# Attention on one core: the order of a round's instructions, and eight sets of split heads

## The chip, the cores and the metric

One NeuronCore of a Trainium2 chip. The metric is the device time of one execution in microseconds (us). Five engines work beside each other, each in the order of its own instruction stream: TensorE (PE, with its weight loads shown as PEld), VectorE (DVE), ScalarE (ACT), GpSimd (POOL) and SyncE (SP, which only issues DMAs here). Semaphores tie them together where one reads what another writes.

## The reference

Attention with 4 batches, 8 heads, 576 positions, 64 dimensions a head; then a mixture of eight experts with the two best per token, then a dense layer pair with a leaky activation.

```python
scores = scale * np.matmul(q, k.transpose(0, 1, 3, 2))
thresh = np.max(scores, axis=-1, keepdims=True) - tau
scores = np.where(scores >= thresh, scores, -1000000000.0)
attn = np.exp(scores - max); attn = attn / (sum + 1e-09)
x = np.matmul(attn, v)                          # 2304 tokens x 512
x = sum over the two best experts of weight * (relu(x @ w1[e]) @ w2[e])
h = x @ w_in
out = (max(h, 0) + alpha * min(h, 0)) @ w_out
```

## The kernel before, in words

Heads go in pairs: the two heads of a pair fill the 128 partitions, 64 each. Attention is cut into 80 units of (batch b, row block c, head pair hp). A full unit is 128 query rows of two heads, so it has two score matrices of 128 x 576; a "t" unit is the last or first 64 rows of both heads put in one 128-row matrix. Units 0 to 15 are batch 0 by head pair, then by block; after them a tile of 128 tokens takes four consecutive units, one for each head pair. Units 16 to 23 and 56 to 63 are the "t" units.

Scores are computed from q and k split into a high and a low part (fp32r), three products each (`s_mm`, L333 to L347). The split parts of one head pair are a *set*; `split_hi` (L285, ScalarE copy), `split_lo` (L293, GpSimd subtraction in two halves, and for q the four small copies of `tail_tile`, L277) fill it. Six sets lie in six buffers; the list `sched` (L639 to L648) says at which round each part is split, and after each split the next raw part is loaded by a DMA on SP (`next_load`).

A unit goes through these steps:

- scores on TensorE into the PSUM ring `s` (two buffers, one for each head);
- `d1` (L358) on VectorE: scale, write to SBUF, row minimum of the negated scores;
- `a1` (L369) on ScalarE: the exponential; `thresh` (L363): the threshold;
- `d2` (L382) on VectorE: the mask times the exponential, with its row sum;
- `t_mm` (L399 to L403) on TensorE: transposes of 4, 4 and 1 blocks into the PSUM ring `t` (three buffers); `a2` (L411 to L415) on ScalarE: copies of them to SBUF;
- `pv` on TensorE into the single PSUM buffer `v`: 16 products on half the array's columns (L434) and one on the whole array for the last 64 positions (L436); for "t" units L429 and L430.

The order is written out by hand in one loop (L714 to L757). Round i issues the scores, `d1`, `a1` and `thresh` of unit i, `d2` of unit i-1, transposes and copies of unit i-2 and `pv` of unit i-3. When the fourth head pair of a tile is done, its result is copied out (`group_evac`, L460), and in the following rounds come the tile's stages: rows (four transposes L475, then on VectorE an addition, a reciprocal and the scaling L471 to L477, and a DMA), logits (L485 and the copy L488), flip (one transpose L492), and the sum of the logits (L496 and L499 on VectorE). All but the sum stand at the end of a round (phase 1); the sum stands at phase 0. They use the ring `t` too. Later rounds hold the gating of two or three tiles at a time (L520 to L576), and the sends of tokens by GpSimd's DMAs (L594).

From round 66 on the first expert's weights are split in the same loop (L170, L173). After the last unit, pieces of the first expert block (`do_fill`) fill the drain. The expert layers that follow are TensorE products in three terms (L197, L215).

Of the kernel before, what the change touches and what calls it, by code (L numbers as in the profile page):

```python
# [4 lines left out]
FT = mybir.dt.float32  # L5
FR = mybir.dt.float32r
# [8 lines left out]
HP = H // 2  # L15
# [8 lines left out]
NSET = 6  # L24
DT = 2
# [7 lines left out]
def emit(tc, qt, kt, v, tau, wg, wn, noise, w1, w2, w_in, w_out, alpha, out):  # L33
# [8 lines left out]
    with (  # L42
# [47 lines left out]
        m_pair = [mem.tile([128, 4096], FR, name=f"m_pair{i}") for i in range(NSET)]  # L90
# [58 lines left out]
        for p, k in ((4, 3), (5, 5), (2, 7), (3, 9), (0, 11), (1, 13)):  # L149
            slots(m_pair[p], k, k + 1)  # L150
# [6 lines left out]
        X0 = (cut(m_pair[0], 0, [HP, 256], FR), cut(m_pair[0], 1024, [HP, 256], FR))  # L157
        H0 = (cut(m_pair[0], 2048, [8 * 256], FR), cut(m_pair[1], 0, [8 * 256], FR))
# [108 lines left out]
        def pair(n):  # L267

            c = Cuts(m_pair[n % NSET])
            return [c([S], FR), c([S], FR), c([KW], FR), c([KW], FR), c([128], FR), c([128], FR)]  # L270
# [148 lines left out]
        def pv(i):  # L419
            b, c, hp = units[i]  # L420
            u = st[i]
            P = u["P"]
            if hp == 0 or i < SOLO:
                vps["v"] = psum_v()
            o = vps["v"][:, hp * 128:hp * 128 + 128]
            V, BD = vt[b % 2], vbd[b % 2]
            if c == "t":
                for j in range(4):
                    pe.matmul(o, V[:, j, hp * 128:hp * 128 + 128], P[:, j], start=(j == 0), stop=False)  # L429
                pe.matmul(o, V[:64, 4, hp * 128:hp * 128 + 128], P[:64, 8], start=False, stop=True)  # L430
            else:
                for j in range(4):
                    for h in range(2):
                        pe.matmul(o[h * 64:h * 64 + 64], V[:, j, hp * 128 + h * 64:hp * 128 + h * 64 + 64],  # L434
                                  P[:, 4 * h + j], start=(j == 0), stop=False, skip_group_check=True)
                pe.matmul(o, BD[:, hp], P[:, 8], start=False, stop=True, skip_group_check=True)  # L436
            st[i].clear()
# [203 lines left out]
        for b in range(1, B):  # L641
            o = 20 * b
            for j, (dt, part) in enumerate(((-12, "q"), (-10, "k"))):
                sched.append((o + dt, 4 * b, part, pool))
            for j, (dt, part) in enumerate(((-8, "q"), (-6, "k"))):
                sched.append((o + dt, 4 * b + 1, part, pool))
            sched += [(o - 4, 4 * b + 2, "q", pool), (o - 3, 4 * b + 2, "k", pool),
                      (o - 1, 4 * b + 3, "q", pool), (o, 4 * b + 3, "k", pool)]  # L648
            put(o - 9, load_v, b)
# [63 lines left out]
        END = NU + DT + 1  # L713
        for i in range(END):  # L714
            it = i - DT
            tiles = 0 <= it < NU
            if i < NU:
                s_mm(i)
                for h in range(nh(i)):
                    d1(i, h)  # L720
                for h in range(nh(i)):
                    a1(i, h)
                thresh(i)
            else:
                do_fill()
# [3 lines left out]
            if tiles:  # L729
                t_mm(it, 0)  # L730
                a2(it, 0)
            for f, a in at.pop((i, 0), []):
                f(*a)
# [3 lines left out]
            iv = it - 1  # L737
            if 0 <= iv < NU:
# [12 lines left out]
            if tiles:  # L751
                t_mm(it, 2)
                a2(it, 2)
# [212 lines left out]
        ca, cb, cc = [Cuts(mem.tile([128, 4096], FT, name=f"m_pair{i}")) for i in range(3)]  # L966
# [104 lines left out]
```

## Time and profile before

| what | value |
|---|---|
| median of 3 runs (lowest to highest) | 1247.83 us (1243.76 to 1247.86) |
| profiled execution, its own time | 1247.19 us |
| span of the profile | 1245.1 us |
| TensorE busy | 1189.1 us, 96% of the span |
| VectorE, ScalarE, GpSimd busy | 610.9, 545.3, 510.7 us |
| mean granted TensorE clock | 0.993 |
| a raw k part's load (320 KB), issue to landing | 4.6 us |

How to read it: busy shares are means over stages with different limits, so the rows below are taken by stretch. "Idle before, releaser" is how long an engine stood before an instruction, and what ended it; "issue" means that nothing in the profile did. Matmuls overlap one another, so the start of weight loads (PEld) is the better clock for TensorE's order.

### The profile page before, as it was taken

What the parts mean: (1) busy time and instruction counts of PE and PEld (TensorE: products, weight loads), DVE (VectorE), ACT (ScalarE), POOL (GpSimd) and SP (SyncE); (2) the same over time, 40 slices, a digit from 0 to 9 for tenths busy, and PEclk for the clock granted to TensorE, in tenths of its full rate; (3) what the DMA queues carried; (4) which work ended last, traced back from release to release, by engine and by line L of the source; (5) the groups of instructions that cost most, each with busy time, mean ns of one, the idle gap of its engine ahead of it and who ended that gap; (6) DMA issues with size and microseconds to landing.
All of it is one profiled execution on the core that took longest, in us unless ns stands there. A gap on an engine that the chain in (4) does not pass through costs nothing.

```text
span 1245.1 us, 21730 instructions
## 1 busy us (share of the span) xinstructions
PE 1189.1 (96%) x8422; PEld 1047.5 (84%) x8422; DVE 610.9 (49%) x1413; ACT 545.3 (44%) x1109; POOL 510.7 (41%) x609
## 2 busy tenths in 40 slices
PE   7998888988889999999999999999999999999996
PEld 6887666777678899999999898998998998998995
DVE  7967787778844333333535342352442442442340
ACT  7967667766724444344444354442221221221220
POOL 6542542562333445443544444544431441441330
PEclk9999999999999999999999999999999999999998
DMA  6332222123143655554645455541111110110100
GB/s 206 99 101 91 99 89 72 69 76 121 50 166 132 209 176 182 177 181 175 220 169 201 163 178 170 193 146 51 35 35 34 42 39 23 43 43 18 43 10 19
DMA packets 60603, 135.27 MB, mean 109 GB/s; under 512 B 9680, under 2 KB 10320, under 8 KB 60496
## 3 DMA queue, kind: packets, MB, share of 16 engines
q1 hardware_dynamic: 54448, 114.61, 27.3%
q0 software_dynamic: 5760, 18.88, 4.5%
q8 instruction: 68, 1.11, 0.4%
q14 instruction: 39, 0.32, 0.1%
q10 hardware_dynamic: 288, 0.34, 0.1%
HBM read 93.96 MB, written 39.85 MB: 107 GB/s over the span
## 4 chain that ended last, share of the span: by engine, by line
PE 83%; ACT 5%; DVE 5%; issue 4%; POOL 1%; DMA 1%; SPq 0%; ACTq 0%; DVEq 0%; POOLq 0%
PE ps_t L197 33%; PE ps_s L215 33%; PE ps_s L347 6%; PE ps_t L399 2%; ACT m_hh L369 2%; DVE m_tmp L358 2%; PE ps_v L434 2%; DVE m_hh L382 1%; PE ps_t L186 1%; ACT sm L363 1%; ACT m_tmp L411 1%; PE ps_v L436 1%; PE ps_v L186 1%; ACT m_last L411 1%; PE ps_t L475 1%
## 5 line engine op out<-in xcount | busy, mean ns | idle before, releaser
L215 PE MATMUL ps_s<-m_pair,m_hh 128*128 128x512 f32 x1032 | 338.4, 395 | 0.0
L197 PE MATMUL ps_t<-m_v,m_pair 128*128 128x256 f32 (+1 forms) x2016 | 290.6, 295 | 2.5 <-DVE m_gate L208 2.5
L197 PEld LDWEIGHTS ps_t<-m_v,m_pair 128*128 128x128 f32 x2016 | 275.8, 191 | 3.8 <-DVE m_gate L208 2.7
L215 PEld LDWEIGHTS ps_s<-m_pair,m_hh 128*128 128x128 f32 x1032 | 193.9, 188 | 39.9
L942 POOL TENSOR_TENSOR m_gate<-m_tmp,m_hh 128x256 fp32r<-128x256 f32 x144 | 105.0, 741 | 249.1 <-ACT m_hh L941 248.1
L215 PE MATMUL ps_s<-m_pair,m_gate 128*128 128x512 f32 x516 | 201.7, 391 | 0.0
L173 POOL TENSOR_TENSOR m_pair<-m_v,m_pair 128x1024 fp32r<-128x1024 f32 x55 | 135.7, 2469 | 141.8 <-ACT m_pair L170 128.0
L197 PE MATMUL ps_t<-m_v,m_early 128*128 128x256 f32 (+1 forms) x1152 | 174.8, 296 | 1.3 <-ACT m_v L189 0.8
L197 PEld LDWEIGHTS ps_t<-m_v,m_early 128*128 128x128 f32 x1152 | 161.7, 191 | 3.0 <-ACT m_v L189 1.1
L369 ACT ACTIVATE m_hh<-m_tmp,sm 128x576 f32<-128x576 f32 x144 | 105.4, 774 | 89.6 <-DVE m_tmp L358 89.4
L382 DVE SCALAR_TENSOR_TENSOR m_hh<-m_tmp,sm,m_hh 128x576 f32<-128x576 f32 x144 | 133.2, 957 | 0.0
L358 DVE TENSOR_SCALAR_CACHE_REDUCE m_tmp<-ps_s 128x576 f32<-128x576 f32 x144 | 103.9, 754 | 58.8 <-PE ps_s L347 58.3
L208 DVE SCALAR_TENSOR_TENSOR m_gate<-ps_t,m_hh 128x384 fp32r<-128x384 f32 (+1 forms) x120 | 58.3, 493 | 151.3 <-ACT m_hh L207 151.3
L938 DVE TENSOR_SCALAR m_tmp<-ps_t,alpha_t 128x256 f32<-128x256 f32 x144 | 69.7, 484 | 117.1 <-PE ps_t L197 117.0
L941 ACT CAST m_hh<-m_tmp 128x256 fp32r<-128x256 f32 x144 | 58.0, 406 | 144.9 <-DVE m_tmp L939 144.9
L215 PEld LDWEIGHTS ps_s<-m_pair,m_gate 128*128 128x128 f32 x516 | 97.1, 188 | 18.3 <-DVE m_gate L208 0.2
L347 PE MATMUL ps_s<-m_pair 64*128 64x288 f32 (+1 forms) x864 | 90.2, 321 | 7.1 <-ACT m_pair L628 4.4
L207 ACT ACTIVATE m_hh<-ps_t 128x384 fp32r<-128x384 f32 (+1 forms) x120 | 52.2, 440 | 93.9 <-PE ps_t L197 92.8
L347 PEld LDWEIGHTS ps_s<-m_pair 64*128 64x128 f32 (+1 forms) x864 | 70.2, 195 | 19.4 <-issue 5.6
L399 PE MATMUL ps_t<-ident,m_hh 128*128 128x128 f32 x576 | 82.7, 284 | 1.1 <-ACT m_last L411 0.4
L299 POOL TENSOR_TENSOR m_pair<-m_early,m_pair 128x288 fp32r<-128x288 f32 (+1 forms) x60 | 54.5, 929 | 59.1 <-ACT m_pair L289 37.7
L399 PEld LDWEIGHTS ps_t<-ident,m_hh 128*128 128x128 f32 x576 | 64.4, 143 | 12.8 <-issue 7.4
(200 smaller groups left out, 1435.6 us busy)
## 6 DMA issues: line engine op xcount, KB each, us to landing
m_v<-in_w_dram SPq DMA_DIRECT2D x64, 512.0 KB, 3.9
yg<-m_tmp SPq DMA_DIRECT2D x40, 256.0 KB, 2.6
m_tmp<-in_w_in_dram SPq DMA_DIRECT2D x16, 512.0 KB, 4.9
m_tmp<-in_w_out_dram SPq DMA_DIRECT2D x16, 512.0 KB, 4.7
m_v<-xg SPq DMA_DIRECT2D x20, 256.0 KB, 4.5
m_rows<-xg SPq DMA_DIRECT2D x20, 256.0 KB, 4.1
m_early<-in_kt_dram SPq DMA_DIRECT2D x15, 320.0 KB, 4.6
yg<-m_gate SPq DMA_DIRECT2D x18, 256.0 KB, 2.1
```

The lines of the kernel that those rows point to most:

```text
L173: eng.tensor_tensor(WL[n], wraw.pop(n), f32(WH[n]), op=OP.subtract)
L197: pe.matmul(ps[:, :n], w[wc[d]][:, col:col + 128], x[xx][:, d, :n], start=(k == 0), stop=(k == 11))
L208: dve.scalar_tensor_tensor(hs[1][:, f * n:f * n + n], ps, 0.0, f32(h), op0=OP.max, op1=OP.subtract)
L215: pe.matmul(ps, a[:, o:o + 128], ww[w][:, c:c + 512], start=(f == 0 and k == 0), stop=(f == nf - 1 and k == 2))
L347: pe.matmul(u["ps", h][:, x, :288], lhs, kk[r, o:o + 288], start=(k == 0), stop=(k == 2))
L358: dve.tensor_scalar(u["sp"][:, h].rearrange("p (a b) -> p a b", a=2), ps[:, :, :288], -0.125, None, op0=OP.mult, op1=OP.min, accum_out=u[" ...
L369: act.activation(u["em"][:, h], u["sp"][:, h], AF.Exp, bias=u["sm"][:, h:h + 1], scale=-1.0)
L382: dve.scalar_tensor_tensor(u["em"][:, h], u["sp"][:, h], sm[:, 2 + h:3 + h], u["em"][:, h], op0=OP.is_le, op1=OP.mult, accum_out=acc)
L399: pe.transpose(ps[:, j * 128:j * 128 + 128], emf[:, o + j * 128:o + j * 128 + 128], ident)
L938: dve.tensor_scalar(t_, ps, 0.0, alpha_t[:, f:f + 1], op0=OP.min, op1=OP.mult)
L941: act.copy(h, g_)
L942: pool.tensor_tensor(hl[:, f * 256:f * 256 + 256], g_, f32(h), op=OP.subtract)
```

## The change

Each round is written in another order. The scores of unit i+1 are issued in round i, after the transposes of unit i-2; the first scores stand ahead of the loop. The first four transposes and their copy come first in the round, ahead of the minimum and the exponentials; the other two copies come after the exponentials, and the threshold after those. `pv` is cut in two: its whole-array product (`pv_tail`) starts the accumulation between the second and the last transposes, and the 16 half-array products follow after the next scores. Phase 0 moves behind the scores.

The split parts get eight sets, in one buffer, of 2688 words each; the splits of the later batches are put into earlier rounds, one round or two apart. The weight slots and the first expert block's inputs are laid out anew in the same buffer.

```diff
@@ -21,7 +21,8 @@
 CAP = 640
 TAIL = 512
 KW = S + S - TAIL
-NSET = 6
+NSET = 8
+SETW = 2688
 DT = 2
 BLOCK0 = 256
 FIRST = 12
@@ -87,7 +88,7 @@
                 return self.aps[self.i % len(self.aps)]
 
         m_early = mem.tile([128, 6 * 1024], FT, name="m_early")
-        m_pair = [mem.tile([128, 4096], FR, name=f"m_pair{i}") for i in range(NSET)]
+        m_pair = mem.tile([128, 12 * 2048], FR, name="m_pair")
         m_v = [mem.tile([128, 3072], FT, name=f"m_v{i}") for i in range(2)]
         m_last = mem.tile([128, 2048], FT, name="m_last")
         m_hh = mem.tile([128, 4096], FT, name="m_hh")
@@ -146,16 +147,15 @@
                     WH[n] = cut(t, 2048 * i, [1024], FR)
                     WL[n] = cut(t, 2048 * i + 1024, [1024], FR)
 
-        for p, k in ((4, 3), (5, 5), (2, 7), (3, 9), (0, 11), (1, 13)):
-            slots(m_pair[p], k, k + 1)
+        slots(m_pair, *range(3, 15))
         wraw = {}
         c0 = Cuts(m_v[0])
         raw2 = Ring([c0([1024]) for _ in range(2)])
         rows = [c0([DM]) for _ in range(2)] + [cut(m_rows, DM * i, [DM]) for i in range(2)]
         row_tile = Ring(rows)
 
-        X0 = (cut(m_pair[0], 0, [HP, 256], FR), cut(m_pair[0], 1024, [HP, 256], FR))
-        H0 = (cut(m_pair[0], 2048, [8 * 256], FR), cut(m_pair[1], 0, [8 * 256], FR))
+        X0 = [cut(m_pair, 22 * 1024 + 1024 * i, [HP, 256], FR) for i in range(2)]
+        H0 = [cut(m_pair, 18 * 1024 + 2048 * i, [8 * 256], FR) for i in range(2)]
 
         def w_load(n):
             raw = raw2()
@@ -266,7 +266,7 @@
 
         def pair(n):
 
-            c = Cuts(m_pair[n % NSET])
+            c = Cuts(m_pair, n % NSET * SETW)
             return [c([S], FR), c([S], FR), c([KW], FR), c([KW], FR), c([128], FR), c([128], FR)]
 
         for i in range(NSET):
@@ -416,10 +416,10 @@
 
         vps, xts, esum = {}, {}, {}
 
-        def pv(i):
+        def pv_tail(i):
+
             b, c, hp = units[i]
-            u = st[i]
-            P = u["P"]
+            P = st[i]["P"]
             if hp == 0 or i < SOLO:
                 vps["v"] = psum_v()
             o = vps["v"][:, hp * 128:hp * 128 + 128]
@@ -429,11 +429,17 @@
                     pe.matmul(o, V[:, j, hp * 128:hp * 128 + 128], P[:, j], start=(j == 0), stop=False)
                 pe.matmul(o, V[:64, 4, hp * 128:hp * 128 + 128], P[:64, 8], start=False, stop=True)
             else:
+                pe.matmul(o, BD[:, hp], P[:, 8], start=True, stop=False, skip_group_check=True)
+
+        def pv(i):
+            b, c, hp = units[i]
+            if c != "t":
+                P = st[i]["P"]
+                o = vps["v"][:, hp * 128:hp * 128 + 128]
                 for j in range(4):
                     for h in range(2):
-                        pe.matmul(o[h * 64:h * 64 + 64], V[:, j, hp * 128 + h * 64:hp * 128 + h * 64 + 64],
-                                  P[:, 4 * h + j], start=(j == 0), stop=False, skip_group_check=True)
-                pe.matmul(o, BD[:, hp], P[:, 8], start=False, stop=True, skip_group_check=True)
+                        pe.matmul(o[h * 64:h * 64 + 64], vt[b % 2][:, j, hp * 128 + h * 64:hp * 128 + h * 64 + 64],
+                                  P[:, 4 * h + j], start=False, stop=(j == 3), skip_group_check=True)
             st[i].clear()
 
         def tile_of(i):
@@ -640,12 +646,8 @@
                  (6, 3, "q", pool), (7, 3, "k", pool)]
         for b in range(1, B):
             o = 20 * b
-            for j, (dt, part) in enumerate(((-12, "q"), (-10, "k"))):
-                sched.append((o + dt, 4 * b, part, pool))
-            for j, (dt, part) in enumerate(((-8, "q"), (-6, "k"))):
-                sched.append((o + dt, 4 * b + 1, part, pool))
-            sched += [(o - 4, 4 * b + 2, "q", pool), (o - 3, 4 * b + 2, "k", pool),
-                      (o - 1, 4 * b + 3, "q", pool), (o, 4 * b + 3, "k", pool)]
+            for j in range(8):
+                sched.append((9 + j if b == 1 else o - 17 + 2 * j, 4 * b + j // 2, "qk"[j % 2], pool))
             put(o - 9, load_v, b)
         loads = [(n, p) for _, n, p, _ in sched[6:]]
 
@@ -711,31 +713,38 @@
                 f(*a)
 
         END = NU + DT + 1
+        s_mm(0)
         for i in range(END):
-            it = i - DT
-            tiles = 0 <= it < NU
+            it, iv = i - DT, i - DT - 1
+            tiles, outs = 0 <= it < NU, 0 <= iv < NU
+            if tiles:
+                t_mm(it, 0)
+                a2(it, 0)
             if i < NU:
-                s_mm(i)
                 for h in range(nh(i)):
                     d1(i, h)
                 for h in range(nh(i)):
                     a1(i, h)
-                thresh(i)
             else:
                 do_fill()
             if 0 < i <= NU:
                 for h in range(nh(i - 1)):
                     d2(i - 1, h)
-            if tiles:
-                t_mm(it, 0)
-                a2(it, 0)
-            for f, a in at.pop((i, 0), []):
-                f(*a)
             if tiles and nh(it) == 2:
                 t_mm(it, 1)
                 a2(it, 1)
-            iv = it - 1
-            if 0 <= iv < NU:
+            if outs:
+                pv_tail(iv)
+            if tiles:
+                t_mm(it, 2)
+                a2(it, 2)
+            if i < NU:
+                thresh(i)
+            if i + 1 < NU:
+                s_mm(i + 1)
+            for f, a in at.pop((i, 0), []):
+                f(*a)
+            if outs:
                 pv(iv)
                 if units[iv][2] == HP - 1 or iv < SOLO:
                     T = group_evac(iv)
@@ -748,9 +757,6 @@
                                 todo += [(i + {3: 8, NT: 2}.get(t1, 4) + d, p, f) for d, p, f in gating(t0, t1)]
                         for j, p, f in todo:
                             put((j, p), f)
-            if tiles:
-                t_mm(it, 2)
-                a2(it, 2)
             if i >= NU:
                 do_fill()
             for f, a in at.pop((i, 1), []):
@@ -963,7 +969,8 @@
 
 
 
-        ca, cb, cc = [Cuts(mem.tile([128, 4096], FT, name=f"m_pair{i}")) for i in range(3)]
+        m_pair = mem.tile([128, 12 * 2048], FT, name="m_pair")
+        ca, cb, cc = [Cuts(m_pair, 4096 * i) for i in range(3)]
         gw = Ring([ca([1024]) for _ in range(4)])
         gr, gx, gacc = cb([DM]), cb([DM]), cb([DM])
         gt = Ring([cc([DM]) for _ in range(8)])
```

## Rows read from the trace of the kernel before

**Rows 1.** Windows by stretch: length, busy us (count) of each engine, granted clock, DMA share

```profile
19.54:62.57 43.03, 42.96 (x468) 34.65 (x468) 40.15 (x95) 39.71 (x93) 21.95 (x32) 1.00 0.36 107
62.57:90.24 27.67, 26.92 (x242) 23.09 (x240) 18.92 (x51) 18.98 (x50) 13.01 (x31) 1.00 0.35 113
90.24:164.15 73.91, 63.88 (x663) 50.05 (x659) 58.23 (x174) 51.73 (x119) 27.35 (x58) 1.00 0.24 80
164.15:235.87 71.72, 63.86 (x681) 49.78 (x681) 55.71 (x160) 50.27 (x113) 28.66 (x54) 1.00 0.24 85
235.87:262.45 26.58, 25.56 (x230) 22.25 (x228) 17.01 (x56) 16.75 (x44) 16.59 (x40) 1.00 0.23 90
262.45:338.90 76.45, 65.67 (x649) 52.00 (x645) 62.66 (x162) 54.93 (x117) 26.07 (x36) 0.96 0.22 80
```

**Rows 2.** Timeline (start, length, engine, line, [idle before <-releaser]) of a plain unit's weight loads

```profile
44.95 0.82 PEld L347 LDWEIGHTS ps_s<-m_pair 64*128 64x128 f32 x12 [0.17 <-issue]
...
45.94 0.86 PEld L399 LDWEIGHTS ps_t<-ident,m_hh 128*128 128x128 f32 x8 [0.17 <-ACT m_tmp L411]
...
46.97 0.85 PEld L434 LDWEIGHTS ps_v<-m_tmp,m_v 128*64 128x64 f32 x16 [0.17 <-ACT m_pair L291]
...
47.99 0.30 PEld L436 LDWEIGHTS ps_v<-m_tmp,m_v 128*128 128x128 f32 x2 [0.17 <-issue]
...
48.21 0.14 PEld L401 LDWEIGHTS ps_t<-ident,m_hh 128*128 128x128 f32 x1
```

**Rows 3.** Timeline of a unit with a flip, all engines

```profile
173.13 0.82 PEld L347 LDWEIGHTS ps_s<-m_pair 64*128 64x128 f32 x12
...
174.90 0.75 DVE L358 TENSOR_SCALAR_CACHE_REDUCE m_tmp<-ps_s 128x576 f32<-128x576 f32 x1
...
175.02 1.45 ACT L369 ACTIVATE m_hh<-m_tmp,sm 128x576 f32<-128x576 f32 x2 [1.54 <-DVE m_tmp L358]
...
175.57 0.81 DVE L382 SCALAR_TENSOR_TENSOR m_hh<-m_tmp,sm,m_hh 128x576 f32<-128x576 f32 x1
...
176.31 0.82 DVE L382 SCALAR_TENSOR_TENSOR m_hh<-m_tmp,sm,m_hh 128x576 f32<-128x576 f32 x1
...
176.56 1.05 ACT L411 COPY m_tmp<-ps_t 128x512 f32<-128x512 f32 x2
...
177.18 0.14 PEld L401 LDWEIGHTS ps_t<-ident,m_hh 128*128 128x128 f32 x1 [0.72 <-ACT m_tmp L411]
...
177.44 0.82 PEld L347 LDWEIGHTS ps_s<-m_pair 64*128 64x128 f32 x12
```

**Rows 4.** Timeline of a tile's rows stage and the logits after it

```profile
181.49 0.42 PEld L475 LDWEIGHTS ps_t<-ident,m_last 128*128 128x128 f32 x4 [0.66 <-ACT m_last L411]
...
181.57 0.20 DVE L472 RECIPROCAL es<-es 128x8 f32<-128x8 f32 x1
...
182.18 0.69 DVE L477 TENSOR_TENSOR m_gate<-ps_t,es 128x512 f32<-128x512 f32 x1 [0.41 <-PE ps_t L475]
...
186.13 0.16 PEld L485 LDWEIGHTS ps_t<-m_last,m_rows 128*32 128x32 f32 x8 [0.66 <-ACT m_tmp L411]
```

**Rows 5.** Timeline of unit 63's scores, weight loads

```profile
259.51 0.69 PEld L347 LDWEIGHTS ps_s<-m_pair 128*128 128x128 f32 x5 [1.24 <-POOL m_pair L299]
```

**Rows 6.** Timeline of the start, GpSimd

```profile
2.60 4.36 POOL L275 MEMSET m_pair<- 64x64 f32 x24
```

**Rows 7.** Timeline of a masked product beside a GpSimd subtraction

```profile
305.18 2.37 POOL L173 TENSOR_TENSOR m_pair<-m_v,m_pair 128x1024 fp32r<-128x1024 f32 x1 [6.97 <-ACT m_pair L170]
...
306.36 1.81 DVE L382 SCALAR_TENSOR_TENSOR m_hh<-m_tmp,sm,m_hh 128x576 f32<-128x576 f32 x1
```

**Rows 8.** Costliest groups of the page: busy us, mean ns of one, idle before

```profile
L382 DVE SCALAR_TENSOR_TENSOR m_hh<-m_tmp,sm,m_hh 128x576 f32<-128x576 f32 x144 | 133.2, 957 | 0.0
```

**Rows 9.** Timeline of unit 67 and 68, weight loads

```profile
279.07 0.14 PEld L401 LDWEIGHTS ps_t<-ident,m_hh 128*128 128x128 f32 x1 [2.44 <-DVE m_gate L582]
...
280.18 1.46 PEld L347 LDWEIGHTS ps_s<-m_pair 64*128 64x128 f32 x12 [0.33 <-issue]
```

## The prediction

> **What bounds the kernel now.** I read the busy times by stretch first, cut where a unit's scores product begins [rows 1]. The 80 attention units end at 338.9 us; the 906.2 us of the span after that are the two expert layers, which the change leaves alone but for where their weight buffers lie. In attention no engine is full except in the second stretch: TensorE is busy 42.96 of 43.03 us in units 4 to 15, but 63.88 of 73.91 in units 24 to 39, 63.86 of 71.72 in 40 to 55 and 65.67 of 76.45 in 64 to 79. Per unit that is 3.59 us in the full stretch and 4.62, 4.48 and 4.78 in the others.
>
> Next the timeline of a plain unit, weight loads only [rows 2]: scores 0.82, eight transposes 0.86, V product 0.85, its whole-array tail 0.22 (start to start), last transpose 0.14, and 0.17 idle at each of four changes of array shape (64x128, 128x128, 128x64, 128x128, back). The last load ends at 48.35, so the next scores begin at 48.52: 3.57 a unit, all TensorE.
>
> Then a unit that also turns a finished tile around [rows 3]: scores at 173.13, next at 177.44, 4.31. ScalarE's exponentials run from 175.02, the threshold follows them, and only behind it, at 176.56, come the transposes' copies, whose PSUM buffer the round's fourth product through three buffers needs (with the flip ahead of it, that is the last transpose): TensorE stands 0.72 before 177.18. The loop is scores, min, two exponentials, threshold, first copy, last transpose, scores; each unit goes through it once. Units 4 to 15 have no such fourth product, so only they reach 3.57.
>
> **The change, part by part.** All is set against the profiled execution, 1247.19 us (span 1245.1), 0.6 below the median 1247.83; I add that 0.6 at the end by rounding.
>
> *Product tail between transposes.* The shapes become 128x128 (both transposes, tail, last transpose), 64x128 (scores), 128x64 (V): three changes, not four. One 0.17 goes per full unit: 3.57 becomes 3.40. In units 4 to 15, twelve of them, that is 2.0 us. Bounds: nothing, if the change of shape hides behind a wait, and 2.0. I take 2.0, as TensorE is full there.
>
> *Scores one unit ahead, first copy before the exponentials.* This opens the loop. The copy of the first transposes now needs no exponential of its own round, and the min works on scores finished a round earlier. What is late next? First TensorE itself. A tile takes four units and adds its rows (0.42 [rows 4]), logits (0.16 and one more 0.17), and flip (0.14, as a last transpose): 4 x 3.40 + 0.42 + 0.33 + 0.14 = 14.5 us.
>
> Second, VectorE, which runs in order. The rows scaling waits for the rows transposes, which stay at the very end of the round, while the min of the next unit is queued behind it; and the scores after that need the two buffers that this min frees. I lay one round out from the start of its first transposes, at 0. The previous round's scores end 1.19 before 0; a result reaches VectorE 0.27 after the last weight load (181.91 to 182.18 [rows 4]); so the mins start at -0.92. Mins cost 0.67 each and the masked products 0.74 each, start to start [rows 3]: with 0.20 for the reciprocal [rows 4] and as much for the sum's addition ahead of it (an estimate) VectorE is free at 2.3. The rows transposes end at 3.82, the scaling starts at 4.09: 1.8 us idle. Scaling 0.62 (an estimate: its row's 0.69 less the 0.07 by which a masked product's 0.81 exceeds its start to start), two mins, 6.05; the next scores were due at 3.82 + 0.43 + 0.43 + 0.22 + 0.14 + 0.17 = 5.21. TensorE stalls some 0.86. In the other rounds, laid out alike, the mins end 0.8 to 0.9 before they are needed.
>
> Third, the flip's PSUM tile is read by an operation that now stands behind the last transpose, so one of three buffers is held: the last transpose takes the first one again, free at 0.43 + 0.27 + half of the two copies' 1.05 [rows 3] = 1.23, against 0.43 + 0.43 + 0.22 = 1.08 due: 0.15. Together 14.5 + 0.86 + 0.15 = 15.5 a tile, 3.88 a unit, 62.1 per sixteen.
>
> VectorE's own floor is its busy time plus four waits of 1.8: 58.23 + 7.2 = 65.4, 55.71 + 7.2 = 62.9, 62.66 + 7.2 = 69.9 [rows 1]. It is above 62.1 in all three, so I take it: 198.2 against 222.1, a gain of 23.9. Its bounds: no wait at all (58.2, 58.0 and 62.7, TensorE's 14.5 being the bound of the middle one), 43.2; or no gain.
>
> ScalarE issues the same instructions in another order, 51.73, 50.27 and 54.93 us in the three stretches, at most 3.43 a unit [rows 1]: below 3.88, so I cost the reordering at nothing; in the last stretch, where that cover is thinnest, VectorE's 69.9 lies above it anyway.
>
> *Eight sets, splits earlier.* 24 steps move, each with one ScalarE copy, two GpSimd subtractions, for a q part also four GpSimd tail copies, and the next load on the DMA queue of SP, which passes zero fills and row stores there. Loads keep their order and a ring of nine buffers, so I cost the DMAs at nothing; if that cover goes, one unit waits once for a landing. Gained: the splits no longer meet the short "t" units (16 to 23, 56 to 63). There the scores of unit 63 stood 1.24 for a subtraction [rows 5]. I take 1 us for each stretch, 2.0; bounds 0 and 4. Otherwise TensorE is busy 26.92 of 27.67 and 25.56 of 26.58 us there [rows 1], so little more is to win.
>
> *Start and end.* Eight more memsets at 4.36/24 [rows 6] are 1.45 us of GpSimd ahead of the first subtractions; the first four units wait for products rather than for those. I take 0; bounds -1 and +1.5. The drain after unit 79 has the same work; 0, bounds -1.5 and +1.5.
>
> Sum: 1247.2 - 2.0 - 23.9 - 2.0 = 1219.3, so 1220.
>
> *A rule against it.* The masked product (two tensors in SBUF) took 1.81 us while a GpSimd subtraction of 2.37 ran [rows 7], and 957 ns in the mean [rows 8] against 0.81 alone [rows 3]. The Trainium skill, "GPSIMD Engine Reference", section "Key points", says GpSimd shares its SBUF interfaces with VectorE and contends with instructions that have two SBUF inputs; the trace agrees. By it alone VectorE would be the bound everywhere, which is the second rival below.
>
> **The rivals.**
>
> *TensorE alone.* The rows wait is hidden: 58.2 + 58.0 + 62.7 = 178.9, then 1247.2 - 43.2 - 4 = 1200. For it: VectorE runs ahead by most of a round elsewhere. Against it: nothing lets a min pass a waiting scaling.
>
> *GpSimd locks VectorE.* Sixteen subtractions of some 1.6 (two parts each; the nearest row, 2.37, is of a bigger one [rows 7]) and eight of 2.4 make 45 us; the masked products show 144 x (0.957 - 0.815) = 20 of it [rows 8]. If half of the other 25 moves from under the mins onto masked products: 1219.3 + 12 = 1231. For it: the splits now start when the mins are already over. Against it: the mins read PSUM and are not slowed, and waiting for the rows gives room.
>
> *The wait only moves.* The next first transposes need the second copy's buffer, which still stands behind the exponentials. If that is late, 4.31 stays, and only the 4 us remain: 1243. Against it: laid out as above the second copy ends near 3.1 (0.70, two exponentials, two copies), the transposes come at 3.4 to 3.8.
>
> *Slower: the clock falls at each tile.* TensorE stood 2.44 us before 279.07 and the scores behind it took 1.46 instead of 0.82 [rows 9]; the granted clock of that stretch is 0.96 [rows 1], so part of it ran at 1.2 GHz, not 2.4. If the rows stall grows from 0.86 to 2.44, a tile costs 15.5 + 1.6, and one unit at 1.78 times its 0.82 + 2.07 of array work adds 2.2: 19.3, against 222.1/12 = 18.5 now. Twelve tiles: +9.8, less 4, 1253. [...] The Trainium skill, "TensorE: Matmul & The Clock Gate", section "Part 1", says a monitor of recent activity sets this clock; the order of these two rows agrees.
>
> **How the numbers follow.** Forecast 0.52, around 1212 to 1228; TensorE alone 0.16; GpSimd lock 0.17; wait only moves 0.07; clock 0.08. The range 1200 to 1239 leaves out half of the first rival and the last two. Half a percent, 6.2 us, is about what can be told from no change here. Faster: 0.51 + 0.16 + 0.14 + 0.02 = 0.83; same 0.01 + 0.03 + 0.05 = 0.09; slower 0.08.
>
> **What would show it.** Units 4 to 15 at 3.40 with three shape changes. In units 24 to 55 about 3.9 to 4.1 a unit, VectorE idle some 1.8 us before each row scaling for TensorE's rows, and a TensorE stall of nearly 1 us before scores once a tile, ended by a min. No copy behind a threshold in front of a last transpose. The stretch behind attention unchanged at about 906 us. I am wrong if TensorE's stalls are at the first transposes instead, if masked products average over 1.1 us, or if the granted clock in units 24 to 79 is below 0.95.

## The result, and the profile after

The changed kernel takes 1217.12 us (median of 4 runs, 1216.08 to 1219.92) against 1247.59 us for the kernel before: a ratio of 0.9766, 95% interval 0.9741 to 0.9792. The profiled run took 1216.61 us with a span of 1214.8 us, 30.3 less than before, at a mean granted clock of 0.996.

Below, the windows of the kernel after, cut where [rows 1] cuts them: units 0 to 3, 4 to 15, the "t" units 16 to 23, units 24 to 39, 40 to 55, the "t" units 56 to 63, then units 64 to 79 as far as the first product of the expert block (310.78 us).

```profile
4.44:18.08 13.64, 11.98 (x69) 9.42 (x69) 9.42 (x26) 8.58 (x18) 12.02 (x38) 1.00 0.79 252
18.08:58.52 40.44, 40.44 (x469) 34.55 (x468) 38.12 (x99) 39.64 (x94) 25.68 (x38) 1.00 0.52 156
58.52:85.33 26.81, 26.81 (x249) 23.51 (x247) 19.00 (x50) 19.69 (x49) 9.77 (x23) 1.00 0.20 67
85.33:148.78 63.45, 60.27 (x644) 49.20 (x643) 54.46 (x169) 51.40 (x117) 36.45 (x65) 1.00 0.33 109
148.78:214.90 66.12, 61.59 (x687) 50.30 (x686) 56.53 (x166) 51.74 (x113) 32.32 (x57) 1.00 0.23 79
214.90:241.76 26.86, 26.76 (x245) 23.12 (x243) 18.03 (x59) 19.70 (x48) 12.68 (x34) 1.00 0.26 99
241.76:310.78 69.02, 63.52 (x659) 51.28 (x659) 62.70 (x162) 55.01 (x116) 25.86 (x36) 1.00 0.26 89
```

TensorE is now full in units 4 to 15 and in the first "t" stretch, and stands 3.2, 4.5 and 5.5 us in the three stretches with tiles (units 24 to 39, 40 to 55, 64 to 79), where it stood 10.0, 7.9 and 10.9: the first two from [rows 1], the third for the kernel before as far as its own first expert product, 66.18 us busy of 77.11. In that last stretch the granted clock also rose, from 0.96 to 1.00. Attention is where the time was won. Stretch by stretch, in us (the last row of attention runs to the first product of the expert block, 339.56 us before, 310.78 after):

| stretch | before | after | change | forecast |
|---|---|---|---|---|
| units 0 to 3 | 15.10 | 13.64 | -1.5 | 0 |
| 4 to 15 | 43.03 | 40.44 | -2.6 | -2.0 |
| t 16 to 23 | 27.67 | 26.81 | -0.9 | -1.0 |
| 24 to 39 | 73.91 | 63.45 | -10.5 | -8.5 |
| 40 to 55 | 71.72 | 66.12 | -5.6 | -8.8 |
| t 56 to 63 | 26.58 | 26.86 | +0.3 | -1.0 |
| 64 to first expert product | 77.11 | 69.02 | -8.1 | -6.6 |
| rest of the span | 905.54 | 904.02 | -1.5 | 0 |

The cuts are scores products, and these now run one round earlier, so a piece of each change at a border belongs to its neighbour. The remainder of the span lay between 902.3 and 906.2 in the kernels run below, whatever was changed in attention.

A plain unit after, weight loads (compare [rows 2]):

```profile
28.42 0.83 PEld L347 LDWEIGHTS ps_s<-m_pair 64*128 64x128 f32 x12 [0.17 <-DVE m_hh L382]
29.41 0.85 PEld L441 LDWEIGHTS ps_v<-m_last,m_v 128*64 128x64 f32 x16 [0.16 <-issue]
30.43 0.86 PEld L399 LDWEIGHTS ps_t<-ident,m_hh 128*128 128x128 f32 x8 [0.17 <-ACT m_tmp L413]
31.25 0.30 PEld L432 LDWEIGHTS ps_v<-m_tmp,m_v 128*128 128x128 f32 x2
31.48 0.14 PEld L401 LDWEIGHTS ps_t<-ident,m_hh 128*128 128x128 f32 x1
31.79 0.83 PEld L347 LDWEIGHTS ps_s<-m_pair 64*128 64x128 f32 x12 [0.17 <-DVE m_hh L382]
```

There are three idle pieces of 0.16 to 0.17 instead of four, and 3.37 from scores to scores instead of 3.57.

A unit with a tile's rows, TensorE and VectorE (compare [rows 4]):

```profile
185.10 0.42 PEld L481 LDWEIGHTS ps_t<-ident,m_hh 128*128 128x128 f32 x4 [0.17 <-ACT m_last L413]
...
185.79 0.69 DVE L483 TENSOR_TENSOR m_gate<-ps_t,es 128x512 f32<-128x512 f32 x1 [1.50 <-PE ps_t L481]
...
186.40 0.75 DVE L358 TENSOR_SCALAR_CACHE_REDUCE m_tmp<-ps_s 128x576 f32<-128x576 f32 x1
...
187.07 0.75 DVE L358 TENSOR_SCALAR_CACHE_REDUCE m_tmp<-ps_s 128x576 f32<-128x576 f32 x1
...
187.21 0.18 PEld L347 LDWEIGHTS ps_s<-m_pair 64*128 64x128 f32 x1 [0.49 <-DVE m_tmp L358]
...
187.89 0.83 PEld L347 LDWEIGHTS ps_s<-m_pair 64*128 64x128 f32 x11 [0.49 <-DVE m_tmp L358]
```

VectorE stands 1.50 in front of the scaling; the two mins queued behind it each free a scores buffer 0.49 too late, 0.98 together. This is the stall that the forecast laid out as 0.86.

The round with the flip, weight loads (compare [rows 3], where the last transpose waited 0.72 behind the threshold):

```profile
177.32 0.14 PEld L498 LDWEIGHTS ps_t<-ident,m_rows 128*128 128x128 f32 x1 [0.17 <-issue]
178.00 0.86 PEld L399 LDWEIGHTS ps_t<-ident,m_hh 128*128 128x128 f32 x8 [0.54 <-ACT m_last L411]
178.83 0.30 PEld L432 LDWEIGHTS ps_v<-m_last,m_v 128*128 128x128 f32 x2
179.46 0.14 PEld L401 LDWEIGHTS ps_t<-ident,m_hh 128*128 128x128 f32 x1 [0.34 <-ACT m_tmp L411]
```

Single stands remain: one in units 40 to 55, where a min and the first copy, which both write `m_tmp`, stood 1.83 and 2.31 (their rows name TensorE work that was done by then; which event they waited for stays open), and one at unit 68, where [rows 9] had 2.44:

```profile
160.77 0.76 DVE L358 TENSOR_SCALAR_CACHE_REDUCE m_tmp<-ps_s 128x576 f32<-128x576 f32 x1 [1.83 <-PE ps_t L498]
...
162.51 0.58 ACT L411 COPY m_tmp<-ps_t 128x512 f32<-128x512 f32 x1 [2.31 <-PE ps_v L432]
...
163.14 0.14 PEld L401 LDWEIGHTS ps_t<-ident,m_hh 128*128 128x128 f32 x1 [1.85 <-ACT m_tmp L411]
...
164.39 0.85 PEld L441 LDWEIGHTS ps_v<-m_last,m_v 128*64 128x64 f32 x16 [0.17 <-issue]
...
257.17 0.42 PEld L481 LDWEIGHTS ps_t<-ident,m_hh 128*128 128x128 f32 x4 [0.82 <-ACT m_last L411]
```

The page's groups of the masked products, the mins and the exponentials of the kernel after (busy us, mean ns, idle just before and its main releaser; compare [rows 8]):

```profile
L382 DVE SCALAR_TENSOR_TENSOR m_hh<-m_tmp,sm,m_hh 128x576 f32<-128x576 f32 x144 | 129.7, 933 | 1.4 <-ACT sm L363 1.4
...
L358 DVE TENSOR_SCALAR_CACHE_REDUCE m_tmp<-ps_s 128x576 f32<-128x576 f32 x144 | 103.6, 752 | 24.5 <-PE ps_s L347 22.4
...
L369 ACT ACTIVATE m_hh<-m_tmp,sm 128x576 f32<-128x576 f32 x144 | 105.8, 783 | 11.2 <-DVE m_tmp L358 11.2
```

Mins and exponentials wait far less, 24.5 and 11.2 us: their idle time was 58.8 and 89.6 us before.

### The profile page after: what moved, and what is told of

It is laid out like the page before. It is cut to its first block, busy times and chain, and to the rows that moved or that the text cites. A ratio compares the mean times of both kernels' runs of the same rounds, so it can differ in the third digit from the quotient of the medians.

```text
span 1214.8 us, 21729 instructions
## 1 busy us (share of the span) xinstructions
PE 1177.5 (97%) x8422; PEld 1046.1 (86%) x8422; DVE 603.6 (50%) x1413; ACT 548.9 (45%) x1109; POOL 519.8 (43%) x617
## 4 chain that ended last, share of the span: by engine, by line
PE 89%; DVE 6%; ACT 2%; issue 1%; DMA 1%; POOL 1%; DVEq 0%; POOLq 0%; ACTq 0%
PE ps_t L197 35%; PE ps_s L215 34%; PE ps_s L347 5%; PE ps_v L441 4%; PE ps_t L399 4%; DVE m_tmp L358 2%; DVE m_hh L382 2%; PE ps_t L186 1%; PE ps_v L429 1%; PE ps_v L432 1%; PE ps_v L186 1%; PE ps_s L197 1%; DVE m_gate L483 1%; PE ps_t L481 1%; PE ps_t L401 1%
## 5 line engine op out<-in xcount | busy, mean ns | idle before, releaser
L382 DVE SCALAR_TENSOR_TENSOR m_hh<-m_tmp,sm,m_hh 128x576 f32<-128x576 f32 x144 | 129.7, 933 | 1.4 <-ACT sm L363 1.4
L358 DVE TENSOR_SCALAR_CACHE_REDUCE m_tmp<-ps_s 128x576 f32<-128x576 f32 x144 | 103.6, 752 | 24.5 <-PE ps_s L347 22.4
L369 ACT ACTIVATE m_hh<-m_tmp,sm 128x576 f32<-128x576 f32 x144 | 105.8, 783 | 11.2 <-DVE m_tmp L358 11.2
L347 PE MATMUL ps_s<-m_pair 64*128 64x288 f32 (+1 forms) x864 | 95.2, 320 | 11.2 <-DVE m_tmp L358 6.6
L347 PEld LDWEIGHTS ps_s<-m_pair 64*128 64x128 f32 (+1 forms) x864 | 72.7, 193 | 25.6 <-DVE m_tmp L358 11.8
L399 PE MATMUL ps_t<-ident,m_hh 128*128 128x128 f32 x576 | 81.2, 280 | 2.4 <-ACT m_last L411 1.1
L299 POOL TENSOR_TENSOR m_pair<-m_early,m_pair 128x288 fp32r<-128x288 f32 (+1 forms) x60 | 59.2, 1007 | 41.8 <-ACT m_pair L289 28.6
L399 PEld LDWEIGHTS ps_t<-ident,m_hh 128*128 128x128 f32 x576 | 63.6, 141 | 12.7 <-issue 4.7
```

Of the source, the lines that this page charges most:

```text
L299: pool.tensor_tensor(lo[:, c], raw[:, c], f32(hi[:, c]), op=OP.subtract)
L347: pe.matmul(u["ps", h][:, x, :288], lhs, kk[r, o:o + 288], start=(k == 0), stop=(k == 2))
L358: dve.tensor_scalar(u["sp"][:, h].rearrange("p (a b) -> p a b", a=2), ps[:, :, :288], -0.125, None, op0=OP.mult, op1=OP.min, accum_out=u[" ...
L369: act.activation(u["em"][:, h], u["sp"][:, h], AF.Exp, bias=u["sm"][:, h:h + 1], scale=-1.0)
L382: dve.scalar_tensor_tensor(u["em"][:, h], u["sp"][:, h], sm[:, 2 + h:3 + h], u["em"][:, h], op0=OP.is_le, op1=OP.mult, accum_out=acc)
L399: pe.transpose(ps[:, j * 128:j * 128 + 128], emf[:, o + j * 128:o + j * 128 + 128], ident)
```

## The experiments

Ratios are to the kernel before, run beside each version, with their 95% interval. "Stretch" times are cut as in the table above, each from one profile. "..." marks lines left out of a cut of code or of a view.

**Which part carries it: the copy or the scores.** From the kernel after, the first copy is put back behind the exponentials, the scores staying ahead:

```diff
             if tiles:
                 t_mm(it, 0)
-                a2(it, 0)
...
+            if tiles:
+                a2(it, 0)
...
             if 0 < i <= NU:
```

> The changed kernel with one thing put back: the first copy of the transposes stands behind the two exponentials again; the scores stay one unit ahead. Theory A (the scores ahead open the loop; their min is a round old, so the exponentials start at once and the copy behind them is still early): 1214 to 1221. Theory B (the copy ahead of the exponentials carries half of the gain or more): 1230 or more.

And the other way round, scores back in their own round:

```diff
-        s_mm(0)
...
+            if i < NU:
+                s_mm(i)
...
-            if i + 1 < NU:
-                s_mm(i + 1)
```

> The changed kernel with the other thing put back: each unit's scores at the top of its own round; the copies stay around the exponentials. Theory A (the scores ahead are needed): the exponentials wait for the round's own scores and mins, the second copy comes 1 us later; 4.1 to 4.3 a unit in units 24 to 79, 1228 to 1240. Theory B (the copy order alone opens the loop, and the rows scaling then holds nothing, as the min waits for its scores anyway): 3.8 to 3.9 a unit, 1207 to 1215.

Measured: copy late 1237.44 us, 0.9926 (0.9907 to 0.9946); scores not ahead 1222.21 us, 0.9800 (0.9779 to 0.9822). Taking away the copy's place costs 1.6% (20 us); taking away the scores' place 0.34% (4 us, but the two intervals overlap, so it can't be told from nothing). That lies between the two forecasts for that run and meets neither. With the copy late, units 4 to 15 take 40.52 us (40.44 after), but the three stretches with tiles are 69.1, 73.1 and 78.5. The waits of that kernel from 85 to 320 us (total, times, longest), and one of them in the timeline:

```profile
PEld ps_t L401 <- ACT m_tmp L411: 16.9, 11, 2.1
```

```profile
203.65 1.08 ACT L411 COPY m_tmp<-ps_t 128x512 f32<-128x512 f32 x2
204.29 0.14 PEld L401 LDWEIGHTS ps_t<-ident,m_hh 128*128 128x128 f32 x1 [0.94 <-ACT m_tmp L411]
```

The loop through the exponentials and the copy closes again although the scores are a round ahead. So the copy in front of the exponentials opens it; the scores ahead add little, if anything. Part of the 20 us is the clock: in the three stretches it was granted at 0.98, 0.98 and 0.94, where the kernel after has 1.00, and TensorE was busy 61.70, 62.91 and 66.70 us against 60.27, 61.59 and 63.52 with the same work, 5.9 us in all. (Not ahead, a plain unit takes 3.37 too: the tail between the transposes already leaves three changes of shape.)

**Sets alone, tail alone, order alone.** The kernel before with eight sets and the new split rounds, nothing else:

```diff
-NSET = 6
+NSET = 8
+SETW = 2688
...
-            c = Cuts(m_pair[n % NSET])
+            c = Cuts(m_pair, n % NSET * SETW)
...
+            for j in range(8):
+                sched.append((9 + j if b == 1 else o - 17 + 2 * j, 4 * b + j // 2, "qk"[j % 2], pool))
```

> Eight sets and the earlier splits in the old order. Theory: 1 us in each of the two t stretches and nothing elsewhere, 1245 to 1246; the loop through the exponentials still sets 4.31 a unit. Rival (splits that come just in time cost more than their waits show): 1237 or less.

Measured 1241.78 us, 0.9963 (0.9948 to 0.9978). By the ratio that is 4.6 us, more than the 2.0 foretold, and in its profile it is spread: -1.9 in units 24 to 39, -1.3 in the second t stretch, -2.7 in the rest (which varies by as much).

The kernel before with the product's tail and the last transpose ahead of the half-array products:

```diff
             if 0 <= iv < NU:
+                pv_tail(iv)
+            if tiles:
+                t_mm(it, 2)
+                a2(it, 2)
+            if 0 <= iv < NU:
                 pv(iv)
...
-            if tiles:
-                t_mm(it, 2)
-                a2(it, 2)
```

> The old order but for one thing: the whole-array product and the last transpose stand between the first transposes and the half-array products. Theory: a shape change goes only in rounds without a tile's stage (units 4 to 15), and only there is TensorE the bound: 2 us, 1245 to 1246. Rival (each of 64 full units gains 0.17): 11 us, 1236.

Measured 1266.20 us, 1.0153 (1.0131 to 1.0176): slower by 19 us, where both forecasts had it faster. The shape change does go in plain units, 3.38 instead of 3.57, as in the first two rows (some others of units 4 to 15 take 3.6 to 3.9); but the last transpose has lost the half-array products that stood ahead of it and now meets the late copy uncovered (third row, the waits from 90 to 340 us: total, times, longest; before the change 9.4 us in 13 waits). Here too the clock fell, to 0.94, 0.96 and 0.92 in the three stretches with tiles, from 1.00, 1.00 and 0.96:

```profile
30.24 0.83 PEld L347 LDWEIGHTS ps_s<-m_pair 64*128 64x128 f32 x12 [0.17 <-issue]
...
33.62 0.82 PEld L347 LDWEIGHTS ps_s<-m_pair 64*128 64x128 f32 x12 [0.17 <-issue]
```

```profile
PEld ps_t L401 <- ACT m_tmp L411: 23.3, 12, 1.9
```

The kernel after with six sets, the old split rounds and the tail back in `pv`:

```diff
-NSET = 8
-SETW = 2688
+NSET = 6
...
-            if outs:
-                pv_tail(iv)
```

> The new order of the round with six sets, the old split rounds, and the whole-array product left behind the half-array ones. Theory (the order carries the gain): the tail, last in the round, stands beside the next round's transposes, so there are three shape changes too; only the 2 us of the sets are lost: about 1219 to 1221, ratio to the kernel before 0.977 to 0.979. Rival (the sets and earlier splits carry a third or more): 1227 or more.

Measured 1226.86 us, 0.9843 (0.9821 to 0.9864). A plain unit takes 3.42: with the scores between last transpose and half-array products, the tail at their end borders on the next transposes, so it saves the same change of shape there. That misses the 1219 to 1221 foretold and all but meets the rival's 1227. Of what is missing against the kernel after, 0.8% or 10 us, its profile has 5.1 us in the two t stretches (29.56 and 29.21), where the sets, asked a round earlier, are not ready at their end. Another 5.2 us are in units 24 to 39 (68.60), where no wait names a subtraction: their cause, and how the 10 us divide between the sets and the tail's place, stay open. Weight loads at the end of the first t stretch:

```profile
84.15 1.01 PEld L347 LDWEIGHTS ps_s<-m_pair 128*128 128x128 f32 x5 [2.04 <-POOL m_pair L299]
85.07 1.85 PEld L429 LDWEIGHTS ps_v<-m_last,m_v 128*128 128x128 f32 x8
```

TensorE stands 2.04 for a GpSimd subtraction, and then runs at half clock: the granted clock is 0.57 from 84 to 88 us, and eight loads of L429 take 1.85, where they take 0.97 at full clock.

**VectorE's wait behind the rows.** The rows stage moved ahead in its round (phase 0), for all tiles:

```diff
-            return [(0, 1, rows), (1, 1, logits), (2, 1, flip), (3, 0, sum_)]
+            return [(0, 0, rows), (1, 1, logits), (2, 1, flip), (3, 0, sum_)]
```

> The changed kernel with a tile's rows stage one place earlier in its round: behind the scores, ahead of the half-array products, instead of at the end. Theory (VectorE's wait for the rows transposes stalls TensorE once a tile): the scaling can start 1.0 us earlier, the stall of about 1.0 before the next scores goes, one shape change of 0.17 comes: 12 tiles at 0.7 to 0.85, 8 to 10 us, 1207 to 1209. Rival (VectorE is full, or GpSimd holds it): the wait moves and 1216 to 1219 stays.

Measured 1216.34 us, 0.9748 (0.9722 to 0.9773): no real gain. Units 40 to 55 fell from 66.12 to 61.24, but the last stretch rose from 69.02 to 75.18. There, in the timeline:

```profile
290.75 2.34 POOL L173 TENSOR_TENSOR m_pair<-m_v,m_pair 128x1024 fp32r<-128x1024 f32 x1 [0.96 <-ACT m_pair L170]
290.82 2.31 DVE L560 TENSOR_TENSOR m_gate<-m_gate 128x24 bf16<-128x24 f32 x1
...
293.06 0.74 DVE L358 TENSOR_SCALAR_CACHE_REDUCE m_tmp<-ps_s 128x576 f32<-128x576 f32 x1
...
293.86 0.18 PEld L347 LDWEIGHTS ps_s<-m_pair 64*128 64x128 f32 x1 [2.66 <-DVE m_tmp L358]
...
295.69 1.57 PEld L441 LDWEIGHTS ps_v<-m_tmp,m_v 128*64 128x64 f32 x16 [0.29 <-issue]
```

A VectorE addition of 24 columns lasted as long as the GpSimd subtraction beside it; the mins behind it were late, TensorE stood 2.66, and then ran at half clock (granted 0.54 from 295 to 298 us; 1.57 for a V product of 0.85). Two trials followed, with the first weight subtractions on VectorE instead of GpSimd, without and with the rows moved:

```diff
-            put(i + 1, w_lo, n, pool if n < 6 else dve)
+            put(i + 1, w_lo, n, dve)
```

> The changed kernel with the six weight subtractions of the first expert that ran on GpSimd in units 67 to 77 put on VectorE. Theory (a GpSimd subtraction holds VectorE's operations on SBUF for its whole 2.4 us; the same work on VectorE takes 1.22 as the last two show): units 64 to 79 get 4 to 6 us shorter, 1211 to 1214. Rival (VectorE only loses its own time, the hold is small): 1.22 x 6 = 7 us longer, 1222 to 1225.

> The rows stage ahead of the half-array products, as in the run before that moved it, and the six weight subtractions on VectorE. Theory (moving the rows gained 5.5 us in units 24 to 55 and lost it again behind two GpSimd holds in units 64 to 79): both gains stand, 1204 to 1209. Rival (VectorE is full in units 64 to 79 whatever holds it): 1215 or more.

Measured 1217.95 us, 0.9769 (0.9746 to 0.9791), and 1217.45 us, 0.9769 (0.9746 to 0.9792): nothing that can be told from the kernel after, both times; the first meets neither of its forecasts, the second meets its rival's. In the first the masked products did get shorter, a mean of 869 ns where the kernel after has 933, 9.2 us in all:

```profile
L382 DVE SCALAR_TENSOR_TENSOR m_hh<-m_tmp,sm,m_hh 128x576 f32<-128x576 f32 x144 | 120.5, 869 | 1.4 <-ACT sm L363 1.3
```

The last stretch still took 69.81 (69.02 after), its granted clock falling from 1.00 to 0.98. VectorE paid for the shorter products with the six subtractions themselves (1.22 us each, 7.3 us), so this run does not show what the products' wait alone costs. In the second, with rows early, the last stretch took 73.42. TensorE stood there 1.55 behind ScalarE, then 0.76 and 0.49 behind a min that itself had waited 3.07 with no releaser among the core's engines; that one stays open.

Rows early for the tiles up to unit 55 alone:

```diff
+            return [(0, 1 if T >= 14 else 0, rows), (1, 1, logits), (2, 1, flip), (3, 0, sum_)]
```

> The rows' stage is put earlier in its round for the tiles up to unit 55 alone; later tiles as in the kernel after. If the gain of 4.9 us in units 40 to 55 and the loss of 6.2 us behind unit 64, seen with all rows earlier, belong each to their own stretch, the first stays and the second goes: 40 to 55 near 61.2, the last stretch near 69.0, 1211 to 1213. Rival (the loss behind unit 64 comes from being ahead of the weight transfers and GpSimd work by then, not from where the rows stand there): the last stretch near 74 again, 1216 to 1218.

Measured 1214.52 us, 0.9742 (0.9722 to 0.9762). The last stretch is back at 69.83, so its loss does come from where the rows stand there; units 40 to 55 took 63.39. (With all rows early, the same order in that stretch, they took 61.24: single profiles differ by that much.) It has the lowest ratio of all, but its interval and that of the kernel after overlap: it can't be called faster. At unit 68 it shows the same fall of the clock, after a stand of 1.70:

```profile
254.14 0.42 PEld L481 LDWEIGHTS ps_t<-ident,m_hh 128*128 128x128 f32 x4 [1.70 <-ACT m_last L411]
...
256.28 1.57 PEld L399 LDWEIGHTS ps_t<-ident,m_hh 128*128 128x128 f32 x8 [0.33 <-issue]
```

The wait itself taken away, by splitting the rows stage in two rounds:

```diff
+                ps = g["rows"] = psum_t()
...
+            def scaled():
+                e, ps = esum[T], g["rows"]
...
-                ps = psum_t()
...
+            return [(0, 1, rows), (1, 0, scaled), (1, 1, logits), (2, 1, flip), (3, 0, sum_)]
```

> Takes VectorE's wait for the rows away: the rows' transposes stay at the end of their round, and the sum's addition, the reciprocal and the scaling run one round later, behind that round's masked products, when the transposes have long ended. If VectorE's wait behind the rows is what holds a tile at 16.5 us in units 40 to 55 and 64 to 79, the wait of 1.5 us before the row scaling goes, TensorE's stand of about 1 us before the scores behind it goes too, and a PSUM buffer held one round longer costs at most 0.15 a tile: units 24 to 39 stay near 63, 40 to 55 fall from 66.1 to about 61 to 62, and the last stretch from 69.0 to about 66; 1208 to 1211. Rival (a gap is only moved: the transposes that come one round later want the PSUM buffer that the rows hold, or the last stretch loses what the middle gains, as with the rows moved earlier): 1215 to 1219, with TensorE standing 0.5 us or more before first or last transposes in that round.

Measured 1220.2 us, 0.9792 (0.9770 to 0.9813). The scaling waits no more, but the rows hold one of the three transposes' buffers for a round, and the second transposes of that round stand for a copy:

```profile
201.16 0.42 PEld L478 LDWEIGHTS ps_t<-ident,m_tmp 128*128 128x128 f32 x4
...
202.98 0.42 PEld L399 LDWEIGHTS ps_t<-ident,m_hh 128*128 128x128 f32 x4 [0.97 <-ACT m_tmp L411]
...
204.30 0.69 DVE L485 TENSOR_TENSOR m_gate<-ps_t,es 128x512 f32<-128x512 f32 x1
```

From 85 to 310 us, TensorE's waits for mins fell from 9.9 to 5.6 us, while those of the transposes for ScalarE's copies rose from 6.4 to 10.8 (L399 and L401 for L411), and the logits wait 2.5 for the scaling. The stall is moved, not removed: the three stretches took 63.49, 66.05 and 69.70 (63.45, 66.12 and 69.02 after).

**GpSimd beside VectorE.** Each subtraction of a split done twice:

```diff
-                pool.tensor_tensor(lo[:, c], raw[:, c], f32(hi[:, c]), op=OP.subtract)
+                for _ in range(2):
+                    pool.tensor_tensor(lo[:, c], raw[:, c], f32(hi[:, c]), op=OP.subtract)
```

> Each subtraction of a split is done twice on GpSimd, to the same place: twice the time in which GpSimd holds its memory port in attention, nothing else added. If GpSimd's instructions stop VectorE's masked products, some 24 more of 1.6 to 2.4 us, about 45 us in all, each delay a VectorE that has about 5.5 us free per tile: by the share that now falls on masked products (their mean of 0.93 against 0.81 alone, 144 of them, 17 us) another 17 us of VectorE time, of which more than half shows, 1227 to 1235. Rival (VectorE's idle time takes it): 1217 to 1221. If the splits themselves come late instead, TensorE's stands before scores name GpSimd.

Measured 1235.42 us, 0.9903 (0.9885 to 0.9921). Masked products rise to 1038 ns, 15.3 us in all (lines of this kernel are one further down). The time is at the edge of the 1227 to 1235 foretold, but not for the reason given: most of the 18 us is elsewhere, 8.9 in units 4 to 15, where the splits themselves are late, and 5.3 in units 24 to 39, where the sends of tokens stand behind the doubled work on GpSimd and the scaling waits for one of them:

```profile
L383 DVE SCALAR_TENSOR_TENSOR m_hh<-m_tmp,sm,m_hh 128x576 f32<-128x576 f32 x144 | 145.0, 1038 | 0.8 <-ACT sm L364 0.8
```

```profile
22.61 1.22 PEld L348 LDWEIGHTS ps_s<-m_pair 64*128 64x128 f32 x10 [4.69 <-POOL m_pair L300]
...
132.68 0.69 DVE L484 TENSOR_TENSOR m_gate<-ps_t,es 128x512 f32<-128x512 f32 x1 [3.40 <-DMA xg<-m_gate,posi]
...
133.42 0.14 PEld L402 LDWEIGHTS ps_t<-ident,m_hh 128*128 128x128 f32 x1 [2.34 <-DVE m_gate L484]
```

In units 40 to 55 neither happens: products 3.1 us longer, the stretch 1.1. By this one pair of profiles a little over a third of what GpSimd adds to VectorE there reaches the end.

## Why the prediction was right, step by step

It said 1220 us and 1217 came, with 23.9 us from the three stretches where 24.2 came. The loop that it named was there and was opened, and the stall that it laid out is in the trace. That the sum agrees so closely is luck: stretch by stretch it missed by -2.0, +3.2 and -1.5 us, and the term that set it, VectorE's floor, did not bound the kernel. The terms one by one:

- **Tail between transposes, -2.0 in units 4 to 15.** Mechanism right: three changes, 3.37 a unit (forecast 3.40), -2.6 in the stretch. But the term is not the tail's own: with the tail alone a plain unit gets the 3.38 and the kernel loses 19 us, and in the new order the tail saves nearly as much where it was (3.42). The bound "nothing" from below was too kind; alone it costs.
- **Scores ahead and first copy: the loop opened.** Right, but the forecast took the two for one edit. The copy carries 20 us of it, the scores at most about 4, not clear of noise.
- **The wait for the rows.** Right in place and releaser, too large in size: twelve waits of 1.8 us were forecast for the three stretches, 21.6 us. Measured were 1.6 us in 2 waits, 5.4 in 4 and 1.0 in 1, together 8.0 us. TensorE's stall was forecast as 0.86 (the forecast's own terms give 6.05 - 5.21 = 0.84) against 0.98 in the timeline shown, and its stands for mins were 3.6, 3.7 and 2.8 us, changes of shape included, against 3.4 forecast a stretch.
- **VectorE's floor.** That VectorE's busy time plus four waits ends the stretches does not hold. The forecast had 65.4, 62.9 and 69.9. With the waits as measured it would be 54.46 + 1.6 = 56.1, 56.53 + 5.4 = 61.9 and 62.70 + 1.0 = 63.7, all below the stretches' 63.45, 66.12 and 69.02. VectorE did idle 9.0, 9.6 and 6.3 us, about as much as the 7.2 put down for it, but most of that was other waits. TensorE was busy 95, 93 and 92% of the stretches. The chain of work that ended last runs through its instructions for 72% of units 40 to 55, but for 30 and 51% of the two others, so what bounds those stays open. TensorE's own path was forecast as 62.1 a stretch, also too short: in 40 to 55 it stood 2.6 for the last transpose and 1.2 for the scaling's buffer, against 4 x 0.15 forecast for buffers. The one stand of 1.85, whose first cause is open, is half of that.
- **Sets: -2.0.** Measured alone 4.6; in the new order they are worth 10 us together with the tail's place, of which 5.1 us lie where scores one round ahead need the splits one round sooner. The forecast's price stood for a kernel in which the old splits still kept up; with the order alone the time is 1226.9. From before to after, in the t stretches themselves only 0.6 came: TensorE is full there now (26.81 of 26.81, 26.76 of 26.86).
- **Start and end: 0.** -1.5 each. At the start most is the cut: the kernels with scores ahead show 13.0 to 13.7 there, those without 14.5 to 15.1.

The rivals. *TensorE alone* (1200) is out: taking the wait away only moved it. *GpSimd locks VectorE* (1231): the hold shows in the trace, the price does not. The products' mean fell from 957 to 933 ns instead of rising. (Six of the weight subtractions ran on GpSimd, not eight, so the forecast's 45 us should have been 40.) *The wait only moves* (1243): in the flip's round 0.54 and 0.34 stand where 0.72 stood, but in the other rounds it is small: from 85 to 310 us the first and second transposes waited 4 times for the copy of a buffer in `m_last`, 1.9 us in all. *The clock falls at each tile* (1253): no; the rows' stall came as two of 0.49, and the granted clock is 1.00 in all stretches. The mechanism is real, though: versions with stands of 1.7 to 2.7 us show the fall, and it is part of what the late copy and the tail alone cost.

## What to carry to other kernels

When one engine's loop runs through several others, look first at the in-order queue in the middle of it: a copy that frees a buffer, issued ahead of work of its own round, was worth 20 us here, computing the input a round ahead at most some 4. A step that saves time in plain rounds can lose far more in the rounds with an extra buffer user, so lay out the fullest round before pricing it. And an order that asks for inputs earlier needs the depth of those inputs' buffers raised with it; price the two together.

## What the runs showed of the hardware

- A VectorE addition of 128x24 elements, 0.18 us otherwise, took 2.31 us beside a GpSimd subtraction of 2.34: the length of the hold is GpSimd's instruction, not VectorE's. In the kernel after, four masked products, 0.81 us alone, took 2.91 to 2.93 beside subtractions of 2.38 to 2.60. The Trainium skill, "GPSIMD Engine Reference", section "Key points", has VectorE instructions with two SBUF inputs contend with GpSimd for the shared interface; the first of these rows agrees, and shows that size is no protection.
- After stands of 2.04, 2.66 and 1.70 us TensorE ran at 1.2 GHz for a while (eight loads of L429 1.85 instead of 0.97, a V product 1.57 instead of 0.85, eight transposes 1.57 instead of 0.86), while after the stand of 1.85 at 163.14 the V product at 164.39 took 0.85. The length of one stand alone does not decide it here.
